# Attention and a gated feed-forward in one kernel: token units of 256 and 512 in place of 256, 320 and 448, with the early plan redone

## The chip, the cores and the metric

The kernel runs on one core of a Trainium2 chip. The metric is the device time of one execution in microseconds (us). A core has a matrix engine (TensorE, PE in the profile, with its weight loads as PEld), a vector engine (VectorE, DVE), a scalar engine (ScalarE, ACT), a general engine (GpSimd, POOL) and a queue engine (SyncE, SP) that issues most transfers. They run side by side and wait for each other through semaphores. PE writes its results to PSUM, 8 banks of 512 f32 columns; VectorE and ScalarE take them from there to SBUF.

## The reference

Windowed attention (8 batches, 8 heads, 576 tokens, 64 dimensions per head, a window of 64 tokens) feeds a gated feed-forward with a token shift:

```python
scores = scale * np.matmul(q, k.transpose(0, 1, 3, 2))
mask = (rel >= 0) & (rel < window)                 # rel = query position - key position
scores = np.where(mask, scores, -1000000000.0)
scores = scores - np.max(scores, axis=-1, keepdims=True)
attn = np.exp(scores)
attn = attn / (np.sum(attn, axis=-1, keepdims=True) + 1e-09)
x = heads side by side of np.matmul(attn, v)       # 8 x 576 x 512

x_prev = x one token later, zeros at the start of each batch
xk = mu_k * x + (1.0 - mu_k) * x_prev
xr = mu_r * x + (1.0 - mu_r) * x_prev
k = np.maximum(xk @ w_k, 0.0)                      # 512 -> 1024
v = k * k @ w_v                                    # 1024 -> 512
r = 1.0 / (1.0 + np.exp(-(xr @ w_r)))              # 512 -> 512
return (r * v).astype(np.float32)
```

The weights are float64 and the activations float32; everything is returned in float32.

## The kernel before

**Tiling.** The 8 x 576 tokens are 72 blocks of 64 tokens (`W`, `BLOCKS`). Attention works on groups of two blocks, 36 of them (`GROUPS`, line 26). The feed-forward works on units of blocks (`UNITS`, line 27): unit 0 has 4 blocks (256 tokens), unit 1 has 5 (320), units 2 to 10 have 7 (448). Tokens are the columns of each matmul, so the width of a unit is the width of its matmuls. `FIRST` gives the first block of each unit and `TU` the widest unit. A batch has 9 blocks, so batch boundaries fall inside units; `parts` (line 528) cuts a unit there.

**Attention of a group** (`burst` line 370, `scores` 344, `values` 356, `soften` 443). A burst on PE holds the scores of group g and the products with the values of group g - 1. The scores lie in PSUM tile `s`. VectorE folds the two key blocks of a query block (tile `s`), takes the row maximum (`most`), subtracts it (`pr`); ScalarE takes the exponential; VectorE sums and divides; PE flips the result (`flip`, PSUM tile `t`) and VectorE keeps it twice, masked in two ways (`keep`, tile `pt`, two buffers, so that group g + 1 may be written while group g is read). Groups in `LEAN` leave the subtraction and the sum to ScalarE, by eight exponentials with a bias and an accumulator. `keep_x` (line 426) copies the result of `values` into the unit's tile `xu` on ScalarE: 512 columns at once if both blocks of the group lie in one unit and one batch, in two halves otherwise.

**Feed-forward of a unit.** `mix` (line 537) makes `xk` and `xr` for four chunks of 128 features. For unit 0 (`PE_MIX`) PE does it, with diagonal matrices of the mixing factors (tile `mixer`, made by ScalarE, line 202 and 726); for the others VectorE does it. Each mixed value is kept as two fp32r halves, a high and a low one, and so are the weights, so a product of a 128 x 128 weight takes three matmuls: high by high, high by low, low by high (`product`, line 628). `k_units` makes 8 products over 4 chunks, `r_units` 4 over 4, and `v_units` 4 over 8: 96, 48 and 96 matmuls, 240 in a unit, at any width. Products use three PSUM banks (`m`). `k_units` squares on ScalarE and splits again (`ks`); `r_units` makes the gate in tiles `th` and `r` (four buffers, `R_BUFS`); `v_units` multiplies by the gate on VectorE and stores the rows of a chunk, with one transfer for each batch in it.

**Weights.** Each float64 weight comes as two 32-bit words: 12 chunks of 128 x 512 (first 4 of `w_r`, then 8 of `w_k`) and 16 of 128 x 256 (`w_v`). `decode` (line 232) makes a float32 of it with one step on ScalarE and four on VectorE (tile `wt`), copies the high half on ScalarE and takes the rest either on PE with an identity and a negative identity (chunks in `PE_LOW`: a plain f32 matmul, which the profile shows as two records, and an fp32r one) or by a subtraction on VectorE. `DECODE` holds each chunk's key.

**Order.** Nothing runs in the order of the code. Each step is a `Piece` with an engine, a key (its due time, in steps of six matmuls; a unit has 40), a cost in ns, the pieces that it needs and the buffers that it takes (`Hold`, counted in `room`, line 88). `play` (line 116) goes through time: whenever an engine is free, it takes the piece with the lowest key whose needs are met and whose buffers are free. The order that results is written into the engines' queues, each of which is strict. Keys are given by `BEGIN` (bursts, and the loads two groups ahead), `DECODE` (weights), `MIX_0` and `MIX_1` (the mixing of units 0 and 1 by chunk). `ORDER` is the order of the first loads: `w` is the next weight chunk, `q0` the queries of group 0, a capital `V` a value load in POOL's queue in place of SP's. A transfer's time is computed from its bytes by `RATE`.

Of the kernel before, what the change touches and what calls it, by code (L numbers as in the profile page):

```python
# [10 lines left out]
F32 = mybir.dt.float32  # L11
# [7 lines left out]
P = 128  # L19
# [3 lines left out]
W = 64  # L23
NB = S // W
BLOCKS = B * NB
GROUPS = BLOCKS // 2
UNITS = (4, 5) + (7,) * 9
FIRST = [sum(UNITS[:u]) for u in range(len(UNITS) + 1)]
TU = max(UNITS) * W
NC, NF = DM // P, DF // P  # L30
# [3 lines left out]
R_BUFS = 4  # L34
WC = 512
TB = 6
# [2 lines left out]

STEP = 6  # L40
USTEPS = 40
BEGIN = (-31, -27, -10, 4, 12, 22, 41, 51, 63, 71, 87, 93, 103, 113, 123, 133, 143, 153, 163, 173, 183, 196,
    210, 223, 236, 250, 263, 277, 286, 295, 304, 312, 322, 332, 342, 352)
DECODE = (-31, -28, -23, -22, -18, -11, -7, -7, -5, -1, 0, 3, 7, 8, 9, 10, 11, 12, 12, 14, 15, 16, 17, 21, 19,
    20, 21, 25)
MIX_0 = (-32, -1, 2, 2)
MIX_1 = (29, 32, 40, 55)
PE_LOW = {0, 1, 2, 3, 4, 5, 6, 7, 8, 9, 10, 11, 19}
PE_MIX = {0}
LEAN = {1, 2, 3, 4, 5, 8}  # L50
LOADED = 6
ORDER = (*"w q0 k0 w V0 q1 k1 w w w w w q2 V1 w w k2 V2 w w w q3 w w k3 V3 w w w w w w q4 w w w w w w".split(),
         *"V4 w w q5 k5 V5 k4".split())
LINK = 160
RATE = 370
SLACK = 1500
STEADY = 60
SLACKS = (SLACK,)
# [6 lines left out]
def attn_rwkv_kernel(ctx, tc, qT, kT, v2, mu_k, mu_r, w_k, w_v, w_r, out):  # L65
    nc = tc.nc
    const = ctx.enter_context(tc.tile_pool(name="const", bufs=1))
    ld = ctx.enter_context(tc.tile_pool(name="ld", bufs=2))
    at = ctx.enter_context(tc.tile_pool(name="at", bufs=2))
# [7 lines left out]
    class Engine:  # L77
# [5 lines left out]
        def __getattr__(self, name):  # L83
# [1 line left out]
            return lambda *args, **kw: tc.keep_in_program_order(op(*args, **kw))  # L85

    pe, dve, sca, pool, dma = (Engine(e) for e in (nc.tensor, nc.vector, nc.scalar, nc.gpsimd, nc.sync))
    room = {"tmp": TB, "m": 3, "s": 1, "t": 1, "x": 1, "pr": 2, "sums": 4, "pt": 2, "xu": 2,
            "ks": 8, "r": R_BUFS, "xr": 1, "xk": 1, "q": 2, "k": 2, "v": 3}

    def slow(key):
# [1 line left out]
    pieces = []  # L93
# [22 lines left out]
    def play():  # L116

        left, free, now, begun = {}, {}, 0, []
        for n, p in enumerate(pieces):
            left.setdefault(p.engine, []).append((p.key, n, p))  # L120
            free[p.engine] = 0
        for e in left:
            left[e].sort(key=lambda x: x[:2])
        users = {id(h): len(h.users) for p in pieces for h in p.takes}
        ends = []
        times = [0]
        port, bus, kind = 0, 0, None
        while any(left.values()):
            assert times, [(e, [(p.key, p.fn.__name__) for _, _, p in ps[:4]]) for e, ps in left.items()]
            now = heapq.heappop(times)  # L130
            while times and times[0] == now:
                heapq.heappop(times)
            while ends and ends[0][0] <= now:
                _, _, p = heapq.heappop(ends)
                for hold in (*p.takes, *p.uses):
                    users[id(hold)] -= 1
                    if not users[id(hold)]:
                        room[hold.tag] += 1
            for e, ps in left.items():
                if free[e] > now:  # L140
                    continue
                for i, (_, n, p) in enumerate(ps):
                    if not all(q.done is not None and q.done + (q.lag + p.slack if q.engine != e else 30) <= now
                               for q in p.needs):
                        continue
                    tags = [h.tag for h in p.takes]
                    if any(room[tag] < tags.count(tag) + p.spare for tag in set(tags)):
                        continue
                    del ps[i]
                    for tag in tags:  # L150
                        room[tag] -= 1
                    begin = now
                    if p.port:
                        begin = max(now, port)
                        port = begin + p.cost
                    if e == "PE":
                        begin += TURN.get((kind, p.kind), 0)
                        kind = p.last if hasattr(p, "last") else p.kind
                    free[e] = begin + p.cost
                    p.done = free[e]  # L160
                    if p.size:
                        bus = max((p.done if e == "SP" else begin) + 1900, bus) + p.size / RATE
                        p.lag = max(bus, p.done + 1900) + 500 - p.done
                    begun.append(p)
                    for at in (p.done, p.done + 30, p.done + p.lag):
                        heapq.heappush(times, at)
                    for slack in SLACKS:
                        heapq.heappush(times, p.done + p.lag + slack)
                    heapq.heappush(ends, (p.done + p.lag, n, p))
                    break  # L170
        return begun
# [27 lines left out]
                                pattern=[[1, W]], channel_multiplier=-1)  # L199

    minus = const.tile([P, P], F32R, name="minus")
    mixer = const.tile([P, 2, 2, NC, P], F32, name="mixer")
    muk = const.tile([P, NC], F32, name="muk")
    mur = const.tile([P, NC], F32, name="mur")
    mu1 = const.tile([P, 4, NC], F32, name="mu1")
# [12 lines left out]
    def load_w(count):  # L218
        for n in range(len(raw), len(raw) + count):
            ws, w, i, c, wc = chunks[n]  # L220

            def load(w=w, i=i, c=c, n=n, wc=wc):
                raw[n] = weights_tile(wc, [P, wc, 2], U32)
                dma.dma_start(raw[n].rearrange("p c t -> p (c t)"),
                              w[i * P:(i + 1) * P, c * wc:(c + 1) * wc].bitcast(U32))

            raw.append(None)
            decode(n, transfer(load, 8 * P * wc))

    words = {}  # L230

# [55 lines left out]
    loaded, arrived, held = {}, {}, {}  # L287

    def transfer(fn, size, takes=(), needs=(), key=None, count=1, engine="SP"):
        return Piece(engine, len(pieces) - 9999 if key is None else key, {"SP": 500, "POOL": 1000}[engine] * count, fn,  # L290
                     needs, takes, size=size)

    def load(what, g, key=None, engine="SP"):
        queue = {"SP": dma, "POOL": pool}[engine]
# [36 lines left out]
        count = {"q": 1, "k": 1, "v": 2}[what] * (1 + (b0 != b1))  # L331
        if what == "v":
            count *= 2
        arrived[what, g] = transfer(fn, 5 * P * {"q": 8, "k": 12, "v": 8}[what] * W, [held[what, g]], key=key,
                                    count=count, engine=engine)

    def block(g, s):
# [105 lines left out]
    def soften(key, g, p, bank):  # L443
# [55 lines left out]

        def keep(a):  # L500
            if a == 1:
                sided[g] = at.tile([P, 2, 4, P], F32, name="pt", bufs=2)
            dve.tensor_mul(sided[g][:, a].rearrange("q e (j r) -> q (e j) r", j=2),
                           flipped[g].rearrange("q e (j r) -> q (e j) r", j=2), wide(sides[:, a], 8))

# [31 lines left out]
    def mix(u, c, key, xk, xr):  # L537

        n = UNITS[u] * W
        if u in PE_MIX:  # L540
            for w, (xs, hold, made) in enumerate((xk, xr)):
                ps, bank = [], Hold("m")

                def blended(ps=ps, w=w):
                    ps.append(ps_m.tile([P, 512], F32, name="m", tag="m")[:, :n])
                    (_, _, _, x0), = parts(u)
                    pe.matmul(ps[0], mixer[:, w, 0, c], xs_of[u][:, c, x0:x0 + n], start=True, stop=False)
                    pe.matmul(ps[0], mixer[:, w, 1, c], xs_of[u][:, c, x0 - 1:x0 - 1 + n], start=False, stop=True)

                def high(ps=ps, xs=xs, hold=hold):  # L550
                    if not xs:
                        xs.append(act.tile([P, 2, NC, TU], F32R, name=hold.tag))
                    sca.copy(xs[0][:, 0, c, :n], ps[0])

                def low(ps=ps, xs=xs):
                    dve.tensor_sub(xs[0][:, 1, c, :n], ps[0], xs[0][:, 0, c, :n].bitcast(F32))

                p = Piece("PE", key, 8 * (1.5 + .453 * n), blended,
                          {got[t] for t in range(FIRST[u], FIRST[u + 1])} | {made_mixer[c], mixing.get((u, w))},
                          [bank], [held["x", u]], lag=200, kind="m")  # L560
                mixing[u, w] = p
                p = Piece("ACT", key, acts(n), high, [p], [hold] if c == 0 else [])
                made.append((p, Piece("DVE", key, over(n), low, [p], (), [bank])))
            return
# [157 lines left out]
    def opposite():  # L722
        pool.tensor_scalar(muk1, muk, -1.0, 1.0, op0=ALU.mult, op1=ALU.add)
        pool.tensor_scalar(mur1, mur, -1.0, 1.0, op0=ALU.mult, op1=ALU.add)

    def mixers(c):
        for w, mus in enumerate(((muk, muk1), (mur, mur1))):
            for a, mu in enumerate(mus):
                sca.mul(mixer[:, w, a, c], ident, mu[:, c:c + 1])

    made_minus = Piece("ACT", -99, 200, lambda: sca.mul(minus, ident, -1.0))
    p = Piece("ACT", -98, 200, vectors, lag=2500)
    arrived["mu"] = Piece("POOL", -98, 250, opposite, [p], port=True)
    made_mixer = [Piece("ACT", MIX_0[c] - 1, 800, lambda c=c: mixers(c), [arrived["mu"]]) for c in range(NC)]
    for what in ORDER:
        if what == "w":
            load_w(1)
# [66 lines left out]
```

## Time and profile before

| | |
|---|---|
| time before | 642.08 us, median of 3 runs (641.79 to 642.13) |
| the profiled execution | 642.39 us, its span from the first to the last instruction 640.6 us |
| mean granted PE clock | 0.988 |
| instructions | 14909 |
| transfers | 53.41 MB, 83 GB/s on average |
| product matmuls of 448 columns | 864 for k, 432 for r, 864 for v |
| product matmuls of 320 columns | 96, 48, 96 |
| product matmuls of 256 columns | 96, 48, 96 |

In the profile, an operation is named by the tiles that it writes and reads: `m<-xk,w` are the products of `k_units`, `m<-xr,w` those of `r_units`, `m<-ks,w` those of `v_units`, `s<-k,q` the scores, `x<-pt,v` the products with the values, `t<-ident,pr` the flips, `m<-wt,ident` and `m<-w,minus` a weight's remainder, `m<-xu,mixer` the mixing on PE. All pieces carry line 85, that of the helper which records them, so tiles tell them apart and lines don't. The end of a matmul is modelled, and matmuls overlap: where their rate matters, it is read from one start to the next. An issue on SP that waits (`SPq`) is shown with its waiting time.

### The profile page before, as it was taken

How to read it: one execution, taken by the hardware profiler on the slowest of the kernel's cores; microseconds unless marked ns; L12 is line 12 of the kernel's file. 1: busy time of each engine (PE TensorE's matmuls, PEld its weight loads, DVE VectorE, ACT ScalarE, POOL GpSimd, SP SyncE). 2: the span in 40 equal slices, each digit the busy share in tenths (PEclk: the TensorE clock that was granted, in tenths of full speed). 3: DMA queues.
4: the chain of work that ended last, by engine and by line, in shares of the span. 5: the costliest groups of instructions: out<-in, count | busy, mean ns of one | idle time of the engine just before them, and what ended most of it. 6: DMA issues, size and time to landing. Idle time of an engine off the chain costs nothing.

```text
span 640.6 us, 14909 instructions
## 1 busy us (share of the span) xinstructions
PE 621.4 (97%) x6183; PEld 561.9 (88%) x6183; DVE 432.3 (67%) x921; ACT 357.3 (56%) x802; POOL 20.2 (3%) x55
## 2 busy tenths in 40 slices
PE   4799999999999999999999999999999999999997
PEld 2558999999999999999999999999999999999996
DVE  5899996876696687659457844965795596254211
ACT  3989967546625643663375266346625652672650
POOL 6103000000000000000000000000000000000000
PEclk9699999999999999999999999999999999999999
DMA  8982233231233223313222311241232211001001
GB/s 265 387 268 67 70 93 90 80 96 51 65 118 100 59 64 101 92 36 84 82 58 59 101 45 32 79 140 30 64 119 85 58 33 44 1 1 58 1 0 58
DMA packets 74788, 53.41 MB, mean 83 GB/s; under 512 B 12832, under 2 KB 70688, under 8 KB 74720
## 3 DMA queue, kind: packets, MB, share of 16 engines
q1 hardware_dynamic: 73536, 50.88, 26.0%
q0 software_dynamic: 896, 1.57, 0.9%
q8 instruction: 49, 0.80, 0.5%
q14 instruction: 19, 0.16, 0.1%
q10 hardware_dynamic: 288, 0.00, 0.0%
HBM read 43.00 MB, written 9.44 MB: 82 GB/s over the span
## 4 chain that ended last, share of the span: by engine, by line
PE 87%; DVE 5%; DMA 5%; ACT 2%; issue 1%; SPq 0%; ACTq 0%
PE m L85 75%; PE s L85 5%; PE x L85 4%; DVE wt L85 3%; PE t L85 2%; DMA w<-w_k 2%; DMA w<-w_v 2%; DMA w<-w_r 1%; ACT kf L85 1%; DVE w L85 0%; ACT pr L85 0%; DVE pt L85 0%; DVE most L85 0%; DVE r L85 0%; ACT w L85 0%
## 5 line engine op out<-in xcount | busy, mean ns | idle before, releaser
L85 PE MATMUL m<-xk,w 128*128 128x448 f32 (+2 forms) x1056 | 215.8, 354 | 0.2 <-ACT kf L85 0.2
L85 PE MATMUL m<-ks,w 128*128 128x448 f32 (+2 forms) x1056 | 212.5, 353 | 0.1
L85 PEld LDWEIGHTS m<-ks,w 128*128 128x128 f32 x1056 | 186.5, 188 | 13.4 <-DVE r L85 0.3
L85 PEld LDWEIGHTS m<-xk,w 128*128 128x128 f32 x1056 | 185.9, 188 | 13.6 <-ACT kf L85 0.5
L85 DVE TENSOR_TENSOR ks<-kf,ks 128x448 fp32r<-128x448 f32 (+2 forms) x88 | 52.1, 593 | 100.5 <-ACT ks L85 100.0
L85 PE MATMUL m<-xr,w 128*128 128x448 f32 (+2 forms) x528 | 111.8, 355 | 0.9 <-ACT r L85 0.7
L85 PEld LDWEIGHTS m<-xr,w 128*128 128x128 f32 x528 | 93.9, 188 | 8.6 <-ACT r L85 1.0
L85 ACT ACTIVATE kf<-m 128x448 f32<-128x448 f32 (+2 forms) x88 | 45.9, 522 | 90.3 <-PE m L85 89.1
L85 ACT CAST xk<-e 128x448 fp32r<-128x448 f32 (+1 forms) x40 | 22.4, 560 | 69.4 <-DVE e L85 69.0
L85 DVE SCALAR_TENSOR_TENSOR r<-th,r 128x448 f32<-128x448 f32 (+2 forms) x44 | 26.1, 593 | 42.9 <-ACT r L85 42.8
L85 DVE TENSOR_TENSOR pt<-t,sides 128x512 f32<-128x512 f32 x72 | 48.1, 683 | 9.9 <-PE t L85 9.9
L85 ACT ACTIVATE kf<-kf 128x448 f32<-128x448 f32 (+2 forms) x88 | 48.8, 556 | 2.4
L85 ACT CAST ks<-kf 128x448 fp32r<-128x448 f32 (+2 forms) x88 | 47.8, 544 | 2.5
L85 PEld LDWEIGHTS s<-k,q 64*64 64x64 f32 x1152 | 30.4, 135 | 20.3 <-issue 19.9
L85 PE MATMUL s<-k,q 64*64 64x128 f32 (+1 forms) x1152 | 38.8, 273 | 9.4 <-DMA k<-kT 9.4
L85 DVE SCALAR_TENSOR_TENSOR r<-m,r 128x448 f32<-128x448 f32 (+2 forms) x44 | 25.8, 586 | 24.0 <-PE m L85 23.8
L85 PE MATMUL x<-pt,v 64*64 64x64 f32 x2176 | 39.9, 223 | 1.3 <-DVE pt L85 1.3
L85 PEld LDWEIGHTS x<-pt,v 64*64 64x64 f32 x2176 | 38.1, 139 | 3.3 <-DVE pt L85 1.9
L85 ACT ACTIVATE th<-m 128x448 f32<-128x448 f32 (+2 forms) x44 | 23.0, 523 | 27.4 <-PE m L85 27.1
L85 ACT COPY xu<-x 128x512 f32<-128x512 f32 (+1 forms) x44 | 22.2, 512 | 28.8 <-PE x L85 28.5
L85 ACT CAST xr<-e 128x448 fp32r<-128x448 f32 (+1 forms) x40 | 22.4, 561 | 15.3 <-DVE e L85 15.1
L85 DVE COPY_PREDICATED s<-own,s 128x512 f32<-128x512 uint32 (+1 forms) x44 | 24.0, 545 | 8.6 <-PE s L85 8.2
(63 smaller groups left out, 576.9 us busy)
## 6 DMA issues: line engine op xcount, KB each, us to landing
k<-kT SPq DMA_DIRECT2D x28, 384.0 KB, 3.6
q<-qT SPq DMA_DIRECT2D x32, 256.0 KB, 3.1
v<-v SPq DMA_DIRECT2D x108, 64.0 KB, 2.6
w<-w_k SPq DMA_DIRECT2D x8, 512.0 KB, 13.2
w<-w_v SPq DMA_DIRECT2D x16, 256.0 KB, 6.3
outT<-r SPq DMA_DIRECT2D x12, 224.0 KB, 2.0
w<-w_r SPq DMA_DIRECT2D x4, 512.0 KB, 9.0
k<-kT SPq DMA_DIRECT2D x8, 256.0 KB, 3.3
```

What stands on the lines that cost most here:

```text
L85: return lambda *args, **kw: tc.keep_in_program_order(op(*args, **kw))
```

## The change

The units become two of 4 blocks and eight of 8: ten units in place of eleven, the later ones 512 tokens wide, and each unit begins at a group's first block. The flipped weights (`pt`) have one buffer in place of two. The diagonals for mixing no longer have a tile of their own: they lie in the four buffers of the gate's tile `r`, and are held until unit 0 is mixed. All due times of the early pieces, and of later bursts, are new; so are the sets `PE_LOW` (16 chunks in place of 13) and `LEAN` (group 9 is added) and the order of the first loads (the values of groups 1 to 4 go through SP's queue now). The planner's cost of a transfer is new as well: fixed times by kind in place of bytes by a rate, and a limit of eight transfers under way on SP's queue.

```diff
-UNITS = (4, 5) + (7,) * 9
+UNITS = (4, 4) + (8,) * 8
...
-BEGIN = (-31, -27, -10, 4, 12, 22, 41, 51, 63, 71, 87, 93, 103, 113, 123, 133, 143, 153, 163, 173, 183, 196,
-    210, 223, 236, 250, 263, 277, 286, 295, 304, 312, 322, 332, 342, 352)
-DECODE = (-31, -28, -23, -22, -18, -11, -7, -7, -5, -1, 0, 3, 7, 8, 9, 10, 11, 12, 12, 14, 15, 16, 17, 21, 19,
-    20, 21, 25)
-MIX_0 = (-32, -1, 2, 2)
-MIX_1 = (29, 32, 40, 55)
-PE_LOW = {0, 1, 2, 3, 4, 5, 6, 7, 8, 9, 10, 11, 19}
+BEGIN = (-39.5, -39.0, -7.5, -7.0, 11.5, 16.5, 31.0, 46.5, 64.0, 68.5, 72.0, 79.0, 102.5, 104, 113, 123, 133,
+    143, 152, 162, 172, 182, 191, 201, 211, 221, 230, 240, 250, 260, 269, 279, 289, 298, 308, 318)
+DECODE = (-14.0, -44.5, -28.0, -34.5, -13.0, -21.0, -21.0, -8.5, -10.0, -4.0, -7.5, -1.0, -6.0, 1.5, 3.5,
+    18.0, 0.0, 4.5, 11.0, 20.0, 22.0, 13.5, 25.5, 12.0, 5.0, 28.0, 14.5, 28.0)
+MIX_0 = (-33.0, -8.0, -27.0, -7.5)
+MIX_1 = (42.5, 43.5, 69.5, 96.5)
+PE_LOW = {0, 1, 2, 3, 4, 5, 6, 7, 8, 9, 10, 13, 15, 21, 23, 27}
 PE_MIX = {0}
-LEAN = {1, 2, 3, 4, 5, 8}
+LEAN = {1, 2, 3, 4, 5, 8, 9}
 LOADED = 6
-ORDER = (*"w q0 k0 w V0 q1 k1 w w w w w q2 V1 w w k2 V2 w w w q3 w w k3 V3 w w w w w w q4 w w w w w w".split(),
-         *"V4 w w q5 k5 V5 k4".split())
+ORDER = (*"w k0 q0 v1 w k1 q1 w w w q3 v2 w w w V0 w w w w w w q2 k2 w w w k4 w k3 v3 w w q5 w w V5 w".split(),
+         *"v4 w q4 w w w k5 w".split())
 LINK = 160
-RATE = 370
...
-    room = {"tmp": TB, "m": 3, "s": 1, "t": 1, "x": 1, "pr": 2, "sums": 4, "pt": 2, "xu": 2,
+    room = {"tmp": TB, "m": 3, "s": 1, "t": 1, "x": 1, "pr": 2, "sums": 4, "pt": 1, "xu": 2,
...
-                        bus = max((p.done if e == "SP" else begin) + 1900, bus) + p.size / RATE
-                        p.lag = max(bus, p.done + 1900) + 500 - p.done
+                        if e != "POOL" and len(landed) >= 8 and landed[-8] > begin:
+                            begin = landed[-8]
+                            p.done = free[e] = begin + p.cost
+                        bus = max(p.done + 1900, bus) + p.size
+                        p.lag = max(bus, p.done + 1900) - p.done
+                        if e != "POOL":
+                            landed += [bus] * p.count
...
-    mixer = const.tile([P, 2, 2, NC, P], F32, name="mixer")
...
-            decode(n, transfer(load, 8 * P * wc))
+            decode(n, transfer(load, {512: 1300, 256: 680}[wc]))
...
-                sided[g] = at.tile([P, 2, 4, P], F32, name="pt", bufs=2)
+                sided[g] = at.tile([P, 2, 4, P], F32, name="pt", bufs=1)
...
-                    pe.matmul(ps[0], mixer[:, w, 0, c], xs_of[u][:, c, x0:x0 + n], start=True, stop=False)
-                    pe.matmul(ps[0], mixer[:, w, 1, c], xs_of[u][:, c, x0 - 1:x0 - 1 + n], start=False, stop=True)
+                    for a in range(2):
+                        pe.matmul(ps[0], mixer(w, a, c), xs_of[u][:, c, x0 - a:x0 - a + n], start=a == 0, stop=a == 1)
...
-                          [bank], [held["x", u]], lag=200, kind="m")
+                          [bank], [held["x", u], *mixer_holds[w]], lag=200, kind="m")
...
+    mixer_tiles, mixer_holds = [], [[Hold("r") for _ in range(2)] for _ in range(2)]
+
+    def mixer(w, a, c):
+        return mixer_tiles[2 * w + a][:, c * P:(c + 1) * P]
+
     def mixers(c):
         for w, mus in enumerate(((muk, muk1), (mur, mur1))):
             for a, mu in enumerate(mus):
-                sca.mul(mixer[:, w, a, c], ident, mu[:, c:c + 1])
+                if c == 0:
+                    mixer_tiles.append(tmp.tile([P, NC * P], F32, name="r", bufs=R_BUFS))
+                sca.mul(mixer(w, a, c), ident, mu[:, c:c + 1])
...
-    made_mixer = [Piece("ACT", MIX_0[c] - 1, 800, lambda c=c: mixers(c), [arrived["mu"]]) for c in range(NC)]
+    made_mixer = [Piece("ACT", MIX_0[c] - 1, 800, lambda c=c: mixers(c), [arrived["mu"]],
+                        [h for hs in mixer_holds for h in hs] if c == 0 else []) for c in range(NC)]
```

More of the change, by code (lines that the diff above doesn't have):

```diff
@@ L126, in play @@
         times = [0]
-        port, bus, kind = 0, 0, None
+        port, bus, kind, landed = 0, 0, None, []
         while any(left.values()):
@@ L289, in transfer @@
     def transfer(fn, size, takes=(), needs=(), key=None, count=1, engine="SP"):
-        return Piece(engine, len(pieces) - 9999 if key is None else key, {"SP": 500, "POOL": 1000}[engine] * count, fn,
-                     needs, takes, size=size)
+        p = Piece(engine, len(pieces) - 9999 if key is None else key, {"SP": 480, "POOL": 600, "ACT": 450}[engine] * count,
+                  fn, needs, takes, size=size)
+        p.count = count
+        return p
     def load(what, g, key=None, engine="SP"):
@@ L333, in load @@
             count *= 2
-        arrived[what, g] = transfer(fn, 5 * P * {"q": 8, "k": 12, "v": 8}[what] * W, [held[what, g]], key=key,
+        size = {"q": (920, 1200), "k": (1210, 1600), "v": (920, 1200)}[what][b0 != b1]
+        arrived[what, g] = transfer(fn, size, [held[what, g]], key=key,
                                     count=count, engine=engine)
```

## The prediction

> **What bounds the kernel now.** I read the page first, then the busy times by stretch of the first 140 us, then the chain of waits, then the matrix engine's timeline for start-to-start times. The page:
>
> ```profile
> span 640.6 us, 14909 instructions
> PE 621.4 (97%) x6183; PEld 561.9 (88%) x6183; DVE 432.3 (67%) x921; ACT 357.3 (56%) x802; POOL 20.2 (3%) x55
> ```
>
> PE is the bound on average. The stretches show that this is not so at the beginning (columns: us, busy us and instructions of PE, PEld, DVE, ACT, POOL, clock, DMA share, GB/s):
>
> ```profile
> 0.00:20.00 20.00, 8.76 (x78) 4.50 (x78) 11.59 (x26) 9.69 (x25) 10.24 (x32) 0.86 0.90 283
> 20.00:40.00 20.00, 17.86 (x185) 11.79 (x185) 19.12 (x42) 19.31 (x63) 2.46 (x4) 0.80 1.05 377
> 40.00:60.00 20.00, 18.19 (x185) 14.21 (x186) 19.90 (x59) 16.70 (x56) 4.25 (x8) 1.00 0.44 124
> 60.00:80.00 20.00, 19.75 (x312) 19.05 (x311) 19.79 (x66) 19.86 (x71) 2.57 (x5) 1.00 0.25 63
> 80.00:100.00 20.00, 19.87 (x230) 19.19 (x228) 19.33 (x47) 14.31 (x45) 0.10 (x1) 1.00 0.35 106
> 100.00:120.00 20.00, 20.00 (x302) 19.43 (x301) 13.01 (x25) 14.55 (x47) 0.00 (x0) 1.00 0.21 58
> ```
>
> PE idles 11.2 us in the first 20 us, 2.1 and 1.8 us in the next two, then 0.25 and 0.13, then nothing. VectorE is full from 20 to 100 us (19.1 to 19.9 of 20) and has 7 us to spare from 100 to 120. The granted clock is 0.86 and 0.80 in the first two stretches and 1.00 later. The chain of waits (start, us, what) agrees:
>
> ```profile
> 1.72 0.50 SPq L85
> ...
> 2.26 7.36 DMA w<-w_r
> 9.64 12.95 DMA w<-w_k
> 22.60 10.04 DMA w<-w_v
> 33.04 2.15 DVE wt L85 x5
> ...
> 82.68 3.00 PE m L85 x24
> ...
> 542.12 94.86 PE m L85 x468
> 637.00 0.62 DVE r L85
> ```
>
> So there are three regimes: weights arriving until about 33 us, weight decoding on VectorE until about 82 us, and PE, without a gap, until one gate and one store close the kernel. Whatever shortens PE's stream after 82 us shortens the kernel one for one; a microsecond saved on VectorE before that is worth at most what PE idles there.
>
> **The product matmuls.** A unit of tokens takes 240 product matmuls whatever its width (96 for k, 48 for r, 96 for v). Eleven units (256, 320 and nine times 448 columns) become ten (twice 256, eight times 512): 240 matmuls fewer, the same 4608 columns. What this is worth depends on the start-to-start time ("pitch") at each width, because durations of overlapping matmuls are not additive. Rows of PE's timeline (start, us, what):
>
> ```profile
> 58.44 0.50 PE L85 MATMUL m<-xk,w 128*128 128x256 f32 x3
> ...
> 59.80 1.52 PE L85 MATMUL m<-xk,w 128*128 128x256 f32 x12
> ...
> 116.75 7.21 PE L85 MATMUL m<-ks,w 128*128 128x320 f32 x48
> 123.80 0.60 PE L85 MATMUL t<-ident,pr 128*128 128x128 f32 x4
> ...
> 608.89 7.44 PE L85 MATMUL m<-xr,w 128*128 128x448 f32 x36
> ...
> 616.17 0.77 PE L85 MATMUL m<-ks,w 128*128 128x448 f32 x3
> ```
>
> From 58.44 to 59.80 run four rows of three: 1.36 us over 12, 113.3 ns at 256. From 116.75 to 123.80: 7.05 over 48, 146.9 ns at 320. From 608.89 to 616.17: 7.28 over 36, 202.2 ns at 448. In ns per 64 columns these are 28.3, 29.4 and 28.9: no straight line. No product runs at 512. Two bounds: as two 256s, 226.6 ns; at 448's rate, 8/7 of 202.2, 231.1 ns. One instruction of the same kind does run at 512, the second half of the weight's remainder (a plain f32 product, two records, then one fp32r product):
>
> ```profile
> 36.21 1.03 PE L85 MATMUL m<-xu,mixer 128*128 128x256 f32 x4
> 37.07 1.02 PE L85 MATMUL m<-wt,ident 128*128 128x512 f32 x2
> ...
> 45.37 1.02 PE L85 MATMUL m<-wt,ident 128*128 128x512 f32 x2
> 45.83 0.80 PE L85 MATMUL m<-w,minus 128*128 128x512 f32 x1
> 46.46 1.97 PE L85 MATMUL m<-xu,mixer 128*128 128x256 f32 x8
> ...
> 64.50 0.59 PE L85 MATMUL m<-wt,ident 128*128 128x256 f32 x2
> 64.74 0.47 PE L85 MATMUL m<-w,minus 128*128 128x256 f32 x1
> 65.05 3.69 PE L85 MATMUL m<-xk,w 128*128 128x256 f32 x30
> ```
>
> Two plain products at 256 take 0.86 us (36.21 to 37.07), 0.43 each. The remainder at 256 takes 0.55 (64.50 to 65.05), so its fp32r half takes 0.12, some 7 ns over the pitch of 113. At 512 it takes 1.09 (45.37 to 46.46); less 0.86 that is 0.23, less 7 ns some 0.223, uncertain by 10 ns from rounding. I take 229 ns: inside both bounds and this third reading's error, nearer to 448 as the wider neighbour. Before: 240 x (113.3 + 146.9 + 9 x 202.2) = 499.2 us. After: 240 x (2 x 113.3 + 8 x 229) = 494.1 us. **-5.1 us**, with ends of -9.8 (226.6) and -1.1 (231.1). One ns at 512 is 1.9 us of the kernel.
>
> The Trainium skill (TensorE: Matmul & The Clock Gate, section Back-to-back issue gap) gives a warm gap of N/2.4 + 2.5 ns, a fixed part of 2.5 ns and nothing else that a wider matmul could save; by it this term would be 240 x 2.5 ns, an estimate of -0.6 us, and it speaks against the change. The trace does not agree with its size: it gives 189.2 ns at 448, measured are 202.2.
>
> **Weights' remainders.** PE makes them for 13 chunks now (twelve of 512 columns, one of 256), for 16 after (eleven and five): 11 x 1.09 + 5 x 0.55 - (12 x 1.09 + 0.55) = **+1.1 us** on PE. The four more of 256 belong to the value weights, decoded around 60 to 80 us where PE has 0.25 us free, so nothing covers them; the one of 512 less lies earlier, where it may have been free, which makes +2.2 the other end. VectorE gains 4 x 0.41 and pays one 512-wide subtraction:
>
> ```profile
> L85 DVE TENSOR_TENSOR w<-wt,w 128x256 fp32r<-128x256 f32 x15 | 6.0, 411 | 0.0
> ...
> L85 DVE TENSOR_TENSOR ks<-kf,ks 128x320 fp32r<-128x320 f32 x8 | 3.8, 487 | 1.6 <-ACT ks L85 1.4
> ...
> L85 DVE TENSOR_TENSOR ks<-kf,ks 128x256 fp32r<-128x256 f32 x8 | 3.3, 413 | 0.0
> ```
>
> The subtraction at 512 is about 0.68 (from 413 at 256 and 487 at 320, 1.16 ns a column), so -1.0 us net on VectorE. Unit 1 at 256 in place of 320 takes 74 ns off each of some 32 VectorE operations (16 for mixing, 8 low halves of the squares, 8 for the gate): 2.4 us.
>
> **The early plan.** New keys, chunk order, mixing order and LEAN set move almost every early piece. What they can win is PE's idle time up to 60 us, 15.2 us, of which the first 6.9 are a wait for the first keys:
>
> ```profile
> 6.92 1.56 PE L85 MATMUL s<-k,q 64*64 64x64 f32 x32 [6.92 <-DMA k<-kT]
> ```
>
>  VectorE's relief of about 3 us falls into its full stretch, but PE idles there only 4 us from 20 to 60. I take **-0.5 us**, with ends of -5 and +3: the costs that the planner uses are new too, and an order that fits the chip worse costs as easily. V1 to V4 go from POOL's queue to SP's, sixteen issues ahead of weights:
>
> ```profile
> 5.88 11.13 SPq L85 DMA_DIRECT2D w<-w_k  x8
> ```
>
> SP spends 1.39 us per chunk there, and a single issue takes 0.50 (at 1.72 in the chain), so it waits for the engines and can take the issues in; if not, 16 x 0.5 us would delay weights by parts of 8 us.
>
> **Edits at nothing.** One buffer for flipped weights makes the first write for a group wait until the values of the group before are multiplied. The DVE queue behind it would wait as well. But those products run in the same burst as the group's own scores:
>
> ```profile
> 101.09 1.11 PE L85 MATMUL x<-pt,v 64*64 64x64 f32 x64
> ...
> 108.19 0.69 DVE L85 TENSOR_TENSOR pt<-t,sides 128x512 f32<-128x512 f32 x1 [0.27 <-PE t L85]
> ```
>
> Six us lie between; if the cover were gone, the wait would be at most one burst. The diagonals fill all four gate buffers until unit 0 is mixed. The gate's first write needs a complete r product, which needs the last mix, so the buffers come free first. If the k mix were late, PE would wait for an accumulator. Group 9 becomes lean, which moves a subtraction and a sum from VectorE to sixteen short ScalarE instructions; ScalarE is busy 14.55 of 20 us from 100 on. Units aligned with groups save ScalarE half copies, and batch boundaries now cut seven units in place of six; both engines have room after 100 us.
>
> **Tail.** The last gate and store grow from 448 to 512 columns: 0.62 to about 0.69 us, and the store from 224 to 256 KB:
>
> ```profile
> outT<-r SPq DMA_DIRECT2D x12, 224.0 KB, 2.0
> ```
>
> About 0.1 us more, **+0.15** together.
>
> **Sum.** -5.1 + 1.1 - 0.5 + 0.15 = -4.35 us. The profiled execution took 642.39 us (span 640.6 and 1.8 around it), 0.3 over the median of 642.08; so 638.0 for a like execution and 637.7 us for the median. A difference under 0.2%, 1.3 us, I call the same, which is what measurements of this kernel can tell.
>
> **Rivals.** (1) *Columns cost the same everywhere.* At 512 the pitch is 231.1 ns, products give 1.1 us, remainders take it back: -0.35, 641.7 us. For it: 448 to 512 is a short step and 320 has no better rate than 448. Against: 256 has a better one, and the remainder's rows point to 0.22 or 0.23. Chance 0.13. By the gap rule of the Trainium skill (TensorE: Matmul & The Clock Gate, section Back-to-back issue gap) the sum would be +0.15, an estimate of 642.2 us, which lies with this rival.
>
> (2) *Unit 2 starves.* Unit 1 now gives PE 240 x (146.9 - 113.3) = 8.1 us less work, yet unit 2 still needs all sixteen first blocks. The rows of before:
>
> ```profile
> 114.29 1.11 PE L85 MATMUL x<-pt,v 64*64 64x64 f32 x64
> ...
> 131.93 0.77 PE L85 MATMUL m<-xk,w 128*128 128x448 f32 x3
> ```
>
> The values of the last group that unit 2 needs are multiplied at 114.3, and its first product starts 17.6 us later. If VectorE, full until 100, cannot finish group 7 and the mix any earlier, PE stands for the 8.1 us: -4.35 + 8.1 = +3.7, 645.8 us. It decides from a stall of 4.4 us on. Against it: VectorE has 7 us free from 100 to 120, and is relieved of 3.4. Chance 0.10.
>
> (3) *512 runs at 320's rate*: 235.0 ns, products +6.4 where I have -5.1: +7.2, 649.2 us. For it: from 256 on the rate rises, falls and may rise again, since its cause does not show; against: 512 is two 256s, and the remainder's rows are over 5 ns below. Chance 0.04.
>
> (4) *The new plan recovers a third of PE's early idle time*, 5 us rather than 0.5: 633.2 us. For it: 15 us are there; against: PE has little to do before the first weights, and VectorE's total hardly changes. Chance 0.10.
>
> That the units do not change cannot be; the number of product matmuls shows it at once.
>
> **Numbers.** My forecast has 0.63; its own range is 633.5 to 641.5 (pitch 227 to 231, early plan 2.5 us either way). The range of 8 in 10 is 631.5 to 643.5: it takes in rivals 1 and 4 and the ends of the pitch, and leaves out 2 and 3 (0.14) and the edges. Faster: 0.61 of the forecast, 0.10 of rival 4, 0.04 of rival 1: 0.75. Same: 0.07 of rival 1 and 0.02 of the forecast: 0.09. Slower: rivals 2 and 3 and a rest of rival 1: 0.16.
>
> **What would show it.** In the profile after: 2400 product matmuls; uninterrupted 512-wide rows with a start-to-start time of 227 to 231 ns (over 232.6 would turn the products' term into a loss); PE full from 60 us on, with unit 2's first 512-wide product following unit 1's last within 1 us, and PE's idle time from 0 to 60 us near 15. The forecast is wrong if PE shows a gap between 100 and 130 us, if its idle time before 60 us moves by over 3 us, or if the pitch lies outside its bounds.

## The result and the profile after

The kernel became slower: 649.84 us (median of 4 runs, 648.83 to 649.97) against 641.93 us before, a ratio of 1.0117 with a 95% interval of 1.0102 to 1.0132. The forecast was 637.7 us with a range of 631.5 to 643.5. The profiled execution, 648.83 us, was the fastest of the four; the other three took about 1 us longer.

The page of the changed kernel and its busy times by stretch (columns as in the prediction):

```profile
span 646.7 us, 14353 instructions
PE 625.2 (97%) x5952; PEld 511.8 (79%) x5952; DVE 428.2 (66%) x893; ACT 351.5 (54%) x768; POOL 8.5 (1%) x35
```

```profile
0.00:20.00 20.00, 6.20 (x68) 3.83 (x69) 8.35 (x19) 10.64 (x26) 7.79 (x28) 1.00 0.94 305
20.00:40.00 20.00, 18.63 (x160) 11.77 (x159) 19.93 (x46) 17.34 (x47) 0.00 (x0) 1.00 0.94 319
40.00:60.00 20.00, 19.81 (x232) 16.43 (x232) 19.90 (x57) 17.75 (x65) 0.10 (x1) 1.00 0.38 128
60.00:80.00 20.00, 18.40 (x293) 17.33 (x292) 19.80 (x66) 19.15 (x76) 0.00 (x0) 1.00 0.30 81
80.00:100.00 20.00, 19.86 (x257) 19.23 (x260) 18.85 (x49) 15.15 (x51) 0.11 (x1) 1.00 0.42 120
100.00:120.00 20.00, 19.86 (x328) 19.43 (x321) 15.34 (x36) 15.00 (x50) 0.00 (x0) 1.00 0.31 87
120.00:140.00 20.00, 19.72 (x197) 16.81 (x196) 16.73 (x40) 10.70 (x31) 0.11 (x1) 1.00 0.30 87
```

There are 231 fewer matmul records and 4 us more of matmul time. The early idle time of PE has moved rather than gone: 15.4 us up to 60 us, where it was 15.2, but 2.2 us from 60 to 140 us, where it was 0.4. (The two waits from 60 to 80 us, 0.56 and 1.04 us, are for ScalarE's `kf`.) From 140 us on PE is full in both. So a large part of the loss must lie in the stream itself. PE's timeline late in the kernel, where nothing interrupts it:

```profile
587.22 21.16 PE L84 MATMUL m<-xk,w 128*128 128x512 f32 x90
608.22 0.86 PE L84 MATMUL m<-xr,w 128*128 128x512 f32 x3
```

90 products in 21.00 us: 233.3 ns from start to start, where the prediction had 229 with an upper end of 231.1. The products of the whole kernel by these pitches: 240 x (2 x 113.3 + 8 x 233.3) = 502.3 us against 499.2, +3.1 in place of -5.1. The end of the chain of waits:

```profile
540.29 102.41 PE m L84 x438
642.72 0.69 DVE r L84
```

The last gate starts 4.0 us before the end of the span (646.7), 3.6 before the change. Products +3.1, remainders on PE +1.1, idle time +2.0 and tail +0.4 make 6.6; the span grew by 6.1. The half us between them is not explained. The clock is not shown to do it, although the columns above have 1.00 from 0 to 40 us where the kernel before has 0.86 and 0.80: the records of the clock begin at 29.1 us in this execution, and what lies ahead of them is counted as full. The remainders' plain products show the clock that PE had:

```profile
20.73 1.92 PE L84 MATMUL m<-wt,ident 128*128 128x512 f32 x2
21.65 1.42 PE L84 MATMUL m<-w,minus 128*128 128x512 f32 x1
...
35.45 1.02 PE L84 MATMUL m<-wt,ident 128*128 128x512 f32 x2
35.91 0.80 PE L84 MATMUL m<-w,minus 128*128 128x512 f32 x1
```

From the first row to the second of each pair it is 0.92 us and then 0.46 us, so PE still ran at half speed at 20.7 us here, and by the other pairs at 13.8 and 26.8 us too; before the change the records have half speed from 14.5 to 28.1 us.

### The profile page after: what moved, and what is told of

It is laid out like the page before. It is cut to its first block, busy times and chain, and to the rows that moved or that the text cites. A ratio compares the mean times of both kernels' runs of the same rounds, so it can differ in the third digit from the quotient of the medians.

```text
span 646.7 us, 14353 instructions
## 1 busy us (share of the span) xinstructions
PE 625.2 (97%) x5952; PEld 511.8 (79%) x5952; DVE 428.2 (66%) x893; ACT 351.5 (54%) x768; POOL 8.5 (1%) x35
## 4 chain that ended last, share of the span: by engine, by line
PE 85%; DVE 8%; ACT 3%; DMA 2%; POOL 1%; issue 1%; SPq 0%; POOLq 0%
PE m L84 73%; PE s L84 5%; PE x L84 4%; DVE wt L84 3%; PE t L84 2%; DMA w<-w_k 1%; ACT pr L84 1%; DVE s L84 1%; POOL v L84 1%; DMA k<-kT 1%; ACT r L84 1%; DVE most L84 1%; DVE xk L84 1%; DVE e L84 0%; DVE r L84 0%
## 5 line engine op out<-in xcount | busy, mean ns | idle before, releaser
L84 PE MATMUL m<-xk,w 128*128 128x512 f32 (+1 forms) x960 | 215.6, 375 | 0.8 <-ACT kf L84 0.8
L84 PE MATMUL m<-ks,w 128*128 128x512 f32 (+1 forms) x960 | 213.8, 374 | 0.0
L84 DVE TENSOR_TENSOR ks<-kf,ks 128x512 fp32r<-128x512 f32 (+1 forms) x80 | 51.0, 637 | 102.0 <-ACT ks L84 101.5
L84 PE MATMUL m<-xr,w 128*128 128x512 f32 (+1 forms) x480 | 110.5, 375 | 0.1
L84 ACT ACTIVATE kf<-m 128x512 f32<-128x512 f32 (+1 forms) x80 | 44.3, 560 | 88.2 <-PE m L84 88.1
L84 DVE SCALAR_TENSOR_TENSOR r<-th,r 128x512 f32<-128x512 f32 (+1 forms) x40 | 25.4, 636 | 36.4 <-ACT r L84 36.2
L84 ACT ACTIVATE kf<-kf 128x512 f32<-128x512 f32 (+1 forms) x80 | 47.2, 594 | 2.1
L84 ACT CAST ks<-kf 128x512 fp32r<-128x512 f32 (+1 forms) x80 | 46.2, 581 | 2.2
L84 DVE SCALAR_TENSOR_TENSOR r<-m,r 128x512 f32<-128x512 f32 (+1 forms) x40 | 25.3, 632 | 29.1 <-PE m L84 28.9
L84 ACT ACTIVATE th<-m 128x512 f32<-128x512 f32 (+1 forms) x40 | 22.3, 558 | 23.9 <-PE m L84 23.2
```

## The experiments

Theory 1: the products' start-to-start time ("pitch") at 512 columns is what was mis-sized. Its rival: the early plan or the memory edits cost the time. Four kernels to tell them apart. All were timed against the kernel before on the same chip.

**Halves.** Each 512-wide product becomes two 256-wide ones on the same weights:

```diff
+                step = n // 2 if n == 512 else n
                 for a, e in ((0, 0), (0, 1), (1, 0)):
-                    pe.matmul(ps[0], weight(w, a, c, col), x(c, e), start=(c == 0 and a == e),
-                              stop=(c == count - 1 and a == 1))
+                    for o in range(0, n, step):
+                        pe.matmul(ps[0][:, o:o + step], weight(w, a, c, col), x(c, e)[:, o:o + step],
+                                  start=(c == 0 and a == e and o == 0),
+                                  stop=(c == count - 1 and a == 1 and o + step == n))
```

> The changed kernel with each 512-wide product issued as two 256-wide matmuls on the same weights. If the product term is what was mis-sized (233.3 ns in place of 229) and the pitch belongs to the width, each pair takes 2 x 113.3 = 226.6 ns, and 8 units x 240 x 6.7 ns = 12.9 us go: about 637 us, faster than both kernels. If the loss lies in the early plan and not in the products, or the second weight load is not hidden, it stays at 648 to 651 us or grows.

Measured: 641.5 us, 8.3 less than the change, and no different from before (0.9993, 0.9984 to 1.0002). PE's timeline:

```profile
581.48 20.56 PE L84 MATMUL m<-xk,w 128*128 128x256 f32 x180
601.88 0.84 PE L84 MATMUL m<-xr,w 128*128 128x256 f32 x6
```

20.40 us over 180: 113.3 ns, so a pair takes 226.7 where one wide product takes 233.3. The early plan is untouched and 8.3 us are gone, as much as the whole loss against the kernel before: the products are the cause. Of the expected 12.9 us, 4.6 did not come: between 200 and 500 us, where bursts interrupt the stream, four in ten of the halves start 117 to 119 ns after the one before. After 140 us each uninterrupted row of 20 halves or more, its first ten left out, keeps to one of two pitches: 113.3 ns (27 rows) or 117.8 (26 rows).

**Memory edits alone**, on the kernel before: one `pt` buffer, the diagonals in `r`.

```diff
-    room = {"tmp": TB, "m": 3, "s": 1, "t": 1, "x": 1, "pr": 2, "sums": 4, "pt": 2, "xu": 2,
+    room = {"tmp": TB, "m": 3, "s": 1, "t": 1, "x": 1, "pr": 2, "sums": 4, "pt": 1, "xu": 2,
...
-                sided[g] = at.tile([P, 2, 4, P], F32, name="pt", bufs=2)
+                sided[g] = at.tile([P, 2, 4, P], F32, name="pt", bufs=1)
...
-    mixer = const.tile([P, 2, 2, NC, P], F32, name="mixer")
...
+                    mixer_tiles.append(tmp.tile([P, NC * P], F32, name="r", bufs=R_BUFS))
```

> The kernel before with the memory edits alone: one buffer for flipped weights, the diagonals in the gate's buffers. If these cost nothing, as predicted: 642 us, within 1 us. If the single buffer or the held gate buffers put a wait into the chain, 36 groups x some 0.1 us or a few us at the start: 644 to 648 us.

Measured: 642.35 against 642.17 us (1.0002, 0.9992 to 1.0011). They cost nothing.

**New units, old early plan.** The same, with the units of the change, and the first twelve keys of `BEGIN`, `DECODE`, `MIX_0`, `MIX_1`, `PE_LOW`, `LEAN`, `ORDER` and the transfer costs of before.

```diff
-UNITS = (4, 5) + (7,) * 9
+UNITS = (4, 4) + (8,) * 8
```

> The kernel before with the new units and the memory edits, but with the early plan of before (first 12 burst keys, weight keys, mixing keys, remainder set, lean set, load order and transfer costs). By the product term alone, 240 x (2 x 113.3 + 8 x 233.3 - 2080.0) = +3.1 us: 645 us. If it is near 645, the new early plan costs the other 4 to 5 us of the change; if it is at 650 or over, the old plan fits the new units no better than the new one does, and the plan is no cause.

Measured: 651.93 us (1.0145, 1.0126 to 1.0164; single runs from 649.92 to 652.71), 2.1 more than the change. Its busy times and PE's timeline around the start of unit 2:

```profile
100.00:120.00 20.00, 19.95 (x332) 19.52 (x325) 14.93 (x35) 13.50 (x47) 0.00 (x0) 1.00 0.31 86
120.00:140.00 20.00, 17.35 (x169) 14.00 (x168) 16.95 (x39) 8.32 (x14) 0.10 (x1) 0.83 0.30 89
```

```profile
126.66 3.76 PE L84 MATMUL m<-xk,w 128*128 128x512 f32 x15
132.23 0.49 PE L84 MATMUL m<-xk,w 128*128 128x512 f32 x1 [1.81 <-ACT xk L84]
133.57 3.78 PE L84 MATMUL m<-xk,w 128*128 128x512 f32 x8 [0.84 <-DVE xk L84]
```

Here unit 2 does starve, as the second rival said: its first products wait for the mixed values, PE idles 2.65 us from 120 to 140 and the clock falls to 0.83. The new plan prevents that:

```profile
121.79 1.66 PE L84 MATMUL m<-ks,w 128*128 128x256 f32 x12
123.29 0.86 PE L84 MATMUL m<-xk,w 128*128 128x512 f32 x3
123.99 0.51 PE L84 MATMUL m<-ks,w 128*128 128x256 f32 x3
```

In the change unit 2's first product starts among unit 1's last. The new early plan, its set of remainders included, is worth some 2 us with these units, so going back to the old one would not mend the loss. PE's idle time up to 140 us is 18.6 us with the old plan and 17.5 with the new one, where the kernel before has 15.6: these 2 us come with the new units under both plans.

**The products alone.** A kernel with nothing but products on fixed data, three matmuls for each weight as in `product`, without attention, weights' decoding and outputs; the output rows are filled with the last product.

> Only product matmuls on fixed data, nothing else of the computation, so the start-to-start time at each width stands by itself. Theory A (the pitch belongs to the width): 113 ns at 256, 147 at 320, 202 at 448, 233 at 512, in buffers of any row length (448, 512 or 528 columns), for any order of the three products and for weights that repeat; and a 512-wide product cut into two 256-wide halves takes 2 x 113 = 227 ns. Rival B (the pitch belongs to the buffer: rows of 512 columns lie badly): 448 in rows of 512 columns is slower than 202, and 512 in rows of 528 is faster than 233, about 229. Rival C (the weight load of the following product disturbs it): repeated weights change the pitch.

By the starts in its trace: 120.0 at 256, 146.7 at 320, 173.3 at 384, 206.7 at 448 and 226.7 at 512 with rows of 448 or 512 columns; 202.0 at 448 and 232.0 at 512 with rows of 528. Two rows for 512, the first with weights that repeat, the second in another order:

```profile
182.61 11.07 PE L100 MATMUL s<-xb,w 128*128 128x512 f32 x48
193.52 11.04 PE L100 MATMUL z<-xb,w 128*128 128x512 f32 x48
```

10.91 us over 48, 227.3 ns with the change-over. This fits no theory as stated: no width has the pitch of the kernels but 320, and rows of 528 columns, which B expected to be the faster ones, bring 512 back to 232. A 512-wide product in two halves takes 2 x 120.0 ns here, more than the 226.7 of the whole one, so halving is no remedy in itself. What differs is where in memory the operands lie. In the compiled programs the moving operands of both kernels lie 192 bytes past a multiple of 256, seen from the weights; in rows of 448 or 512 columns of the probe 0 bytes; with 528 columns (64 bytes more in each row) the place changes from row to row. Theory 2, then: the pitch follows from the place of the moving operand.

**The place, alone.** The probe with the first column shifted, and a second set of weights 64 bytes further.

> Product matmuls alone again, on fixed data, with the first column of the moving operand shifted by 0, 4, 8, 12, 16, 24, 32 and 64 f32 columns (4 bytes each), against weights whose address is a multiple of 128 bytes; and three shifts against weights that lie 64 bytes further. Theory D (the pitch follows from where the moving operand lies in a line of 128 bytes): a shift by 16 columns, 64 bytes, gives the pitches of the two kernels (113 at 256, 202 at 448, 233 at 512), a shift by 0, 32 or 64 columns those of the first probe (120, 207, 227). If what counts is the place relative to the weights, weights 64 bytes further swap the two sets; if it is the moving operand alone, they change nothing. Rival (the pitch differs because the other engines are busy in the kernels and idle in the probe): all shifts alike, 120, 207 and 227.

PE's timeline; the places relative to the weights are pa 0, pb 16, pc 32, pd 48, pe 64, pf 96, pg 128, ph 256 bytes, and with the weights `v`, pi 192, pj 224, pk 0:

```profile
121.35 5.12 PE L97 MATMUL pa<-x,w 128*128 128x448 f32 x24
126.30 5.01 PE L97 MATMUL pb<-x,w 128*128 128x448 f32 x24
...
140.97 4.97 PE L97 MATMUL pe<-x,w 128*128 128x448 f32 x24
145.78 5.08 PE L97 MATMUL pf<-x,w 128*128 128x448 f32 x24
...
160.54 5.65 PE L97 MATMUL pa<-x,w 128*128 128x512 f32 x24
166.03 5.72 PE L97 MATMUL pb<-x,w 128*128 128x512 f32 x24
...
182.78 5.67 PE L97 MATMUL pe<-x,w 128*128 128x512 f32 x24
188.29 5.77 PE L97 MATMUL pf<-x,w 128*128 128x512 f32 x24
193.90 5.76 PE L97 MATMUL pg<-x,w 128*128 128x512 f32 x24
199.50 5.62 PE L97 MATMUL ph<-x,w 128*128 128x512 f32 x24
...
213.50 5.02 PE L97 MATMUL pi<-x,v 128*128 128x448 f32 x24
218.36 5.06 PE L97 MATMUL pj<-x,v 128*128 128x448 f32 x24
...
228.22 5.76 PE L97 MATMUL pi<-x,v 128*128 128x512 f32 x24
233.82 5.76 PE L97 MATMUL pj<-x,v 128*128 128x512 f32 x24
239.41 5.62 PE L97 MATMUL pk<-x,v 128*128 128x512 f32 x24
```

From row to row over 24: at 512 columns 228.8 at place 0 (226.7 once settled), 229.6 at 64, 233.3 at 128, 227.1 at 256, 233.3 at 192; at 448 columns 206.3 at 0, 200.4 at 64, 202.5 at 192. The other engines are idle throughout, so they are not the reason. Moving the weights counts as much as moving the operand (from `pa` to `pi` only the weights move, and 512 goes from 228.8 to 233.3): the place is relative. At 192 stand the kernels' pitches at 448 and 512, though not at 256 (118 here, 113.3 in the kernels). Theory D expected the kernels' pitches at 64, and 0 and 128 alike: at 64 stand 229.6 at 512 and 118 at 256, and 0 and 128 differ, so its period of 128 bytes does not hold.

**Moving the operands in the kernels.** The token tile `xu` lies ahead of the product operands, so lengthening its rows moves them all. Three moves of the change, by 64, 128 and 256 bytes, and two of the kernel before:

```diff
-            xs_of[u] = act.tile([P, NC, 2 + TU], F32, name="xu", bufs=2)
+            xs_of[u] = act.tile([P, NC, 4 + TU], F32, name="xu", bufs=2)
```

with 4 + TU for 64 bytes (`e5_shifted`, `e6_before_shifted`), 6 + TU for 128 (`e10_control`, `e13_before_moved`) and 10 + TU for 256 (`e12_control_256`).

> The changed kernel with the token tile two columns longer in each feature chunk, which moves the product operands by 64 bytes, to a multiple of 128, and changes nothing else. Theory D: the pitch at 512 falls from 233.3 to 226.7 ns, that at 256 rises from 113.3 to 120, together 240 x (8 x 6.7 - 2 x 6.7) ns = 9.6 us less: about 640 us, and PE's rows show 226.7. Rival (other engines): no change, 649 to 650 us.

> The kernel before with the same shift by 64 bytes. Theory D: 448 goes from 202.2 to 206.7 ns, 256 from 113.3 to 120, 320 stays: 240 x (9 x 4.5 + 6.7) ns = 11.3 us more, about 653 us. Rival: no change, 642 us.

> Control: the changed kernel with the token tile four columns longer in each chunk, which moves the product operands by 128 bytes, so they lie where they lay in a line of 128 bytes. Theory D: the pitch at 512 stays at 233.3 ns and the time at 649 to 650 us. If any move of the buffers helps (another reason than the place in a line), about 640 us.

> Second control: the changed kernel with the token tile eight columns longer than in the change, which moves the product operands by 256 bytes. Theory E (the pitch follows from the place of the moving operand relative to the weights within 256 bytes, 0, 64, 128 or 192): the place stays at 192, the pitch at 233.3 ns and the time at 649 to 650 us. If any move of the buffers helps, 639 to 642 us, as after the moves by 64 and 128 bytes.

> The kernel before with its product operands moved by 128 bytes, to the place 64. The probe has 200.0 ns there at 448 (202.0 at the place 192), some 118 at 256. Theory E: 240 x (9 x -2.1 + 4.6) ns = -3.4 us: about 638.7 us, and PE's rows show 200 ns at 448. If only 512-wide products depend on the place, 642 us.

| kernel | place | us | ratio to before, 95% |
|---|---|---|---|
| the change | 192 | 649.84 | 1.0117 (1.0102 to 1.0132) |
| the change, 64 further | 0 | 639.34 | 0.9956 (0.9939 to 0.9972) |
| the change, 128 further | 64 | 641.85 | 1.0000 (0.9991 to 1.0009) |
| the change, 256 further | 192 | 648.96 | 1.0107 (1.0092 to 1.0122) |
| before | 192 | 641.93 | |
| before, 64 further | 0 | 644.77 | 1.0040 (1.0025 to 1.0055) |
| before, 128 further | 64 | 637.62 | 0.9930 (0.9915 to 0.9944) |

PE's timeline of the five moved kernels, in the order of the table:

```profile
579.35 20.56 PE L84 MATMUL m<-xk,w 128*128 128x512 f32 x90
599.75 0.84 PE L84 MATMUL m<-xr,w 128*128 128x512 f32 x3
```

```profile
581.30 20.76 PE L84 MATMUL m<-xk,w 128*128 128x512 f32 x90
601.90 0.85 PE L84 MATMUL m<-xr,w 128*128 128x512 f32 x3
```

```profile
587.37 21.16 PE L84 MATMUL m<-xk,w 128*128 128x512 f32 x90
608.37 0.86 PE L84 MATMUL m<-xr,w 128*128 128x512 f32 x3
```

```profile
611.71 7.46 PE L85 MATMUL m<-xr,w 128*128 128x448 f32 x36
619.01 0.77 PE L85 MATMUL m<-ks,w 128*128 128x448 f32 x3
```

```profile
604.13 7.36 PE L85 MATMUL m<-xr,w 128*128 128x448 f32 x36
611.33 0.76 PE L85 MATMUL m<-ks,w 128*128 128x448 f32 x3
```

At 512: 226.7 ns at place 0, 228.9 at 64, 233.3 at 192. At 448: 202.8 at 0, 200.0 at 64, where it was 202.2 at 192. The move by 128 bytes was expected to change nothing and took 8 us off, which refutes a period of 128 bytes; the move by 256 does change nothing, so it is not just any move that helps. One expectation missed in size: the kernel before, 64 further, lost 2.7 us in place of 11.3. Its 448-wide stream does not have one pitch at place 0: of its 44 uninterrupted rows of 20 products or more after 140 us, the first ten of each left out, 32 run at 202.5 to 202.9 ns from start to start and 12 at 206.6 to 206.7, the probe's value, each row keeping to its own. So the place does not settle the pitch alone; what chooses between the two stays open. At 512, and at 448 at the places 192 and 64, all such rows of a kernel agree within 1 ns. Each at the best of these places, the kernel before takes 637.62 us and the change 639.34: the wider units show no gain even then.

**Two places at once.** The shifted change, with the operands of the two 256-wide units 16 or 48 columns into their buffers:

```diff
+    def at_(n):
+        return slice(48, 48 + n) if n == 256 else slice(0, n)
```

> The shifted kernel with the operands of the two 256-wide units put 16 columns into their buffers: each width then lies at the place where it ran fastest, 256 at 113.3 ns and 512 at 226.7. By the pitch alone 2 x 240 x 6.7 ns = 3.2 us less than the shifted kernel's 639.3: 636.1 us. As these units run while VectorE is full, some of it may be taken back as waits: 636 to 639 us.

> The shifted kernel with the operands of the two 256-wide units put 48 columns into their buffers, which gives them the place of 192 that they had in the change. Theory E: 113.3 ns at 256 in place of 120 and 226.7 at 512, 2 x 240 x 6.7 ns = 3.2 us less than the shifted kernel if PE bounds these units: 636.1 us; 636 to 639 if VectorE takes some back.

Measured: 639.0 us with 16 columns, 639.09 with 48, where the shift alone has 639.34. A row of unit 1 in the shifted change, then in the version with 48 columns:

```profile
92.47 5.56 PE L84 MATMUL m<-xk,w 128*128 128x256 f32 x45
97.87 0.60 PE L84 MATMUL t<-ident,pr 128*128 128x128 f32 x4
```

```profile
93.18 5.26 PE L84 MATMUL m<-xk,w 128*128 128x256 f32 x45
98.28 0.60 PE L84 MATMUL t<-ident,pr 128*128 128x128 f32 x4
```

In this row the pitch went from 120.0 to 113.3 ns as expected, and the time did not follow. With 16 columns the place was 64, not the 192 that was wanted, and the pitch 118. With 48 the mean over all products of the two units fell less than in this row, from 119.7 to 115.2 ns, which is 2.2 us for 480 of them. From the first to the last of them PE is busy 1.6 us less and idles 0.4 us more, so some of the gain is waited away, as the expectation said; and in this profiled execution the first of them starts 0.85 us later, after a granted clock of one half that lasted until 31.8 us in place of 28.9. What the places are worth here at an equal start was not measured.

**Remainders.** The change with `PE_LOW` as before:

```diff
-PE_LOW = {0, 1, 2, 3, 4, 5, 6, 7, 8, 9, 10, 13, 15, 21, 23, 27}
+PE_LOW = {0, 1, 2, 3, 4, 5, 6, 7, 8, 9, 10, 11, 19}
```

> The changed kernel with the set of weight remainders on PE as before (13 chunks in place of 16). By the prediction's term, PE is relieved of 1.1 us: 648.7 us. If VectorE is what counts while the value weights are decoded, its extra 1.0 us shows instead: 650 to 651 us.

Measured: 653.04 us, 3.2 more than the change and more than either expectation.

```profile
60.00:80.00 20.00, 16.29 (x200) 15.38 (x199) 19.52 (x64) 17.73 (x73) 0.00 (x0) 0.91 0.32 86
```

PE, freed of the remainders, idles 3.7 us from 60 to 80, where it idled 1.6 in the change. Its own time was not what counted there: from 40 us to 75.0 us, where the longest of these waits ends (2.1 us, for ScalarE's `kf`), the chain of waits runs through VectorE and ScalarE, not through PE. With the new keys and the old set the kernel is no faster than with the old keys and the old set (653.04 against 651.93 us), so no run shows that the new keys are worth anything without the new set.

## Why the prediction was wrong

**The products.** This is the step that failed. "I take 229 ns: inside both bounds": the value was 233.3, outside them, and as "one ns at 512 is 1.9 us of the kernel", the term was 8.2 us off and had the wrong sign. Between the forecast for a profiled execution, 638.0 us, and its 648.83 lie 10.8 us; this term makes 8.2 of them, PE's early idle time 2.5 and the tail 0.3. The bounds rested on the belief that the pitch of a width lies between those of its neighbours, two 256s and 8/7 of 448. It does not, even at one place: both kernels have their products at 192, and there 512 takes 233.3 ns where 8/7 of 448 is 231.1. The runs showed a second variable, the place of the moving operand relative to the weights, which the rows of one kernel cannot show since all its products have the same place. At place 0 the same width takes 226.7 ns, the lower bound. Why 512 takes the most at 192 was not found out. The third reading, the remainder's rows, gave 0.22 to 0.23 us, but for other operands in other buffers.

The third rival had nearly the measured time, 649.2 us, in part by luck: its pitch of 235.0 ns was 1.7 too high, worth 3.2 us, and the 2.5 us of idle time that it did not foresee made up for most of that. Its reason did not hold: at place 0 of the probe 512 takes 226.7 ns where the rate of 320 (146.7) gives 234.7. The first rival's "columns cost the same everywhere" failed as well. The gap rule of the Trainium skill (TensorE: Matmul & The Clock Gate, section Back-to-back issue gap) has N/2.4 + 2.5 ns, 215.8 at 512; none of the places here came under 226.7, so the trace does not agree with it for these products. The section gives it for a single isolated matmul and says that at large widths it counts too much for a stream of weight loads and matmuls, so its own words speak against the use that the prediction made of it; here it counts too little.

**Remainders.** +1.1 us on PE was right as PE's work, wrong as a cost: undoing it made the kernel 3.2 us slower. The prediction said that nothing covers them because PE has 0.25 us free from 60 to 80; but VectorE is as full there (19.8 of 20 us), and the chain of waits runs through it.

**The early plan.** -0.5 was forecast. Idle time grew by 2.0 us up to 140 us, inside the ends given (-5 to +3). Against the old keys and the old set with the same units the new plan saves some 2 us, and unit 2 does not starve with it; as the old set alone costs 3.2 us, the share of the keys is not shown. The second rival did not come true in the change, but with the old plan its place and sign were right. Free time on VectorE, the reason given against it, was not enough: with the old plan VectorE was busy for 14.9 of the 20 us from 100 to 120, and unit 2 starved all the same. Its price was 8.1 us; the idle time from 100 to 140 us, 2.7 us at a lowered clock, was less.

**Edits at nothing** were right as far as they were run, the two memory edits: +0.2 us, inside the interval. **The tail** grew by 0.4 us, not 0.15. **What bounds the kernel** was read rightly: from 140 us on nothing but PE's stream counts, and that is why a few ns at each of 1920 products decided.

**Sums.** Three figures of the prediction do not come out of its own numbers. The pitch at which the products' term turns into a loss is 231.7 ns, not 232.6 (240 x (2 x 113.3 + 8 x 231.7) = 499.2 us), only 0.6 ns over the upper bound. The forecast's own range, 633.5 to 641.5 us, is narrower than its ends added up, 631.3 to 644.0. The subtraction at 512 comes to 0.71 us by 1.16 ns a column, not 0.68; measured are 0.69.

## What to carry to other kernels

Where one engine's stream is the bound, measure the start-to-start time of exactly the instruction that will be new, shape and buffer place both, before its rate is taken from a neighbour. If a change of shape costs more than it should, move the buffers by 64 and 128 bytes before the change is thrown away: here 64 bytes turned +1.2% into -0.4%, and 128 bytes made the kernel before, unchanged otherwise, 0.7% faster, the fastest of all. Try the same moves on the kernel before as well, or the comparison is between places and not between shapes. A microsecond taken off the engine that is full in a stretch can be worth more than one taken off the engine that waits for it: here 1.1 us less work on PE cost 3.2 us.

## What the runs showed of the hardware

The pitch of a product (fp32r operands, a weight load for each) changes with the distance of the moving operand's address from the weights' address, and distances 256 bytes apart gave the same (place 0 and 256 bytes further in the probe, 192 and 256 bytes further in the change): 226.7 to 233.3 ns at 512 columns, 200.0 to 206.7 at 448, 113.3 to 120.0 at 256, and next to nothing at 320 (145 to 147 in the probe). The best place differs from width to width: 0 at 512, 64 at 448, 192 at 256. At two of the places a stream has two pitches and keeps to one of them from one interruption to the next: 202.7 or 206.7 ns at 448 columns and place 0, 113.3 or 117.8 at 256 columns and place 192. After an interruption the pitch takes some five to ten products to settle: in the shifted change, the starts after a burst are 235, 233, 236, 224, 231, 236, 228, 232, 231 ns apart, and then 227 throughout. What in the chip makes the place matter was not found out.
